# Keys and values in three shared 8 KB buffers, gate tiles in the gate buffer, steps 2 and 3 reordered

## The chip, the cores and the metric

The kernel runs on one core of a Trainium2 chip. The metric is the device time of one execution in microseconds (us), the median of several runs. PE is the matrix engine (PEld its weight loads), DVE the vector engine, ACT the scalar engine, POOL the GpSimd engine, SP the queue that issues nearly all DMAs.

## What is computed

Three layers in a row, all in float32:

```
# 1: gated linear attention (mLSTM): batch 2, 8 heads, 768 tokens, head size 40; per token t
m_new  = max(f[t] + m, i[t])
f_stab = exp(f[t] + m - m_new);  i_stab = exp(i[t] - m_new)
C = f_stab * C + i_stab * v[t] k[t]^T          # 40 x 40 state per head
n = f_stab * n + i_stab * k[t]
y[t] = sigmoid(o[t]) * (C q[t]) / max(|n q[t]|, 1)
# 2: soft mixture of experts: x = y as 1536 x 320, 8 experts of 4 slots, hidden size 1024
logits = x @ phi                                # 1536 x 32
slot_input = softmax(logits over tokens).T @ x  # 32 x 320
slot_out[e] = relu(slot_input[e] @ w1[e]) @ w2[e]
x = softmax(logits over slots) @ slot_out
# 3: four experts weighted by domain_probs
out = sum_e p[:, e] * (relu(x @ u1[e]) @ u2[e])
```

## The kernel before

**Layer 1, the attention.** The 768 tokens of each batch are cut into 6 chunks of 128. A token tile i (0 to 11) is chunk `c = i // 2` of batch `b = i % 2`. The recurrence becomes matmuls inside a tile plus a state that goes from chunk to chunk (`state[b]`, one per batch). The order is written out by hand (`manual_schedule`): each engine does its instructions in the order of the code. Tiles 0 and 1 stand in straight code (lines 700 to 771), tiles 2 to 11 in a loop (lines 774 to 884); pass i of the loop is called step i. The stages of a tile that matter here:

- `stage_S` (L337): scores from transposed queries and keys, `stage_E` (L287, L290): decay weights, `stage_mask` (L296, POOL): the triangle, `stage_W` (L343, DVE): their product.
- `stage_P1` (L361): weights times values. `stage_P2` (L353): queries times state. `stage_T2` (L370), `stage_T1` (L377, L379) add them up on DVE; `stage_G`, `stage_N`, `stage_D` normalise and gate (L424, L384 to L387, L430).
- `stage_Wk` (L323, POOL): weighted keys, `stage_V` (L405): their product with the values into the PSUM bank `kv`, `stage_V1` (DVE): that sum into the state, as a copy (L419) for chunk 0 and as an addition (L417) later. `stage_U` (L393, POOL) decays the state.
- `stage_KT` (L304) transposes the keys of tile i+2 in step i. `stage_X` (L438) and `stage_XC` (L443, ACT) transpose the layer's output of tile i-2 for layer 2.
- The gates of chunks 2 and 3 are worked out in steps 1 and 2 by `gates1a` (two scans L602 and L608 with L605 and L606 between), `gates1b` (L625, L628, L633), `gates2` (L648, L650), those of chunks 4 and 5 in steps 3 to 6. `tokT`, `tokC`, `tokM` (L657 to L681) bring them into columns by token.

**Loads.** In step i SP issues the keys of tile i+3, one or two output gates, values of tile i+2 and some rows of the expert weights w1, in the order of the code. Keys, values, output gates and the first queries are loaded per tile as 128 tokens x 8 heads x 40 floats: 1,024 pieces of 160 bytes, 160 KB. Keys go into `kb[i % 4]` with 64 floats per head (24 of padding), values into `vb[i % 4]` with 41 floats per head (a column of ones for the normaliser), output gates into `x1` without gaps. A DMA waits until the eighth before it has landed (eight landing counters, DMAHW0 to 7), and until its target is free.

**Buffers.** `big` has 11 slots of 10 KB. Seven are first taken by `gin` (raw gates), `gt0`, `gt1`, `gt2` (gate work), `qx` (padded queries) and `x1` of the two batches; the tiles w1_0 to w1_3 take the other four, and w1_4 to w1_7, then w2_1, w2_3, w2_5, w2_7 those that come free, in this order. The tiles w2_0, w2_2, w2_4, w2_6 (`slot3`) lie over the memory of the attention's own pools, `ap` and `attw`.

**Layers 2 and 3.** After step 11 the slots are gathered and `ffn1` (L1139, w1) and `ffn2` (L1179, w2) run; SP meanwhile issues the rest of w1, sixteen loads of w2 (L99, 640 KB each) and the first weights of layer 3, u1a, u1b, u2 (L104, L105, L111). Layer 3 begins with `G_mm` (L1248), which needs u1a and u1b, and is then matmuls on PE until the end (L1292, L1308).

Of the kernel before, what the change touches and what calls it, by code (L numbers as in the profile page):

```python
# [8 lines left out]
F32 = mybir.dt.float32  # L9
# [13 lines left out]
def tile_mlstm_soft_moe_domain_moe(  # L23
# [19 lines left out]
    L = 128  # L43
# [15 lines left out]
    def bc(i):  # L59
        return i % B, i // B  # L60
# [4 lines left out]
    def slot(shape, name, dt=F32):  # L65
        return big.tile(shape, dt, tag="w", name=name)
# [58 lines left out]
    with tc.manual_schedule():  # L125
# [10 lines left out]
        with ExitStack() as actx:  # L136
# [1 line left out]
            wp = actx.enter_context(tc.tile_pool(name="attw", bufs=2, side="right", reuse_waits="tile"))  # L138


            NB = 4
            kb = [ap.tile([128, H, 64], F32, name=f"kb{i}") for i in range(NB)]
            wkb = [ap.tile([128, H, 64], F32, name=f"wkb{i}") for i in range(2)]


            EL = ap.tile([128, S], F32R, name="EL")
            ER = ap.tile([128, 4, HP, L], F32R, name="ER")
            eA = ap.tile([128, NC, 4, HP], F32, name="eA")
            wB = ap.tile([128, NC, 4, HP], F32, name="wB")
            dec = ap.tile([128, NC, B, HP], F32, name="dec")  # L150
            rmask = ap.tile([128, 24], F32, name="rmask")
            vb = [ap.tile([128, H * (D + 1) + 24], F32, name=f"vb{i}") for i in range(NB)]
            state = [ap.tile([128, HP, 2, D + 1], F32, name=f"state{i}") for i in range(2)]

            def vbh(i):
                return vb[i % NB][:, 0:H * (D + 1)].rearrange("p (h d) -> p h d", d=D + 1)


            gin = slot([128, 2, S], "gin")[0:16]
            gt0 = slot([128, 3, S], "gt0")  # L160
            gt1 = slot([128, 3, S], "gt1")
            gt2 = slot([128, 3 * S + 256], "gt2")
# [25 lines left out]
            def load_k(i):  # L188
                b, c = bc(i)
                nc.sync.dma_start(  # L190
                    out=kb[i % NB][:, :, 0:D],
                    in_=k[b, :, c * L:(c + 1) * L, :].rearrange("h p d -> p h d"),
                )

            def load_v(i):
                b, c = bc(i)
                nc.sync.dma_start(
                    out=vbh(i)[:, :, 0:D],
                    in_=v[b, :, c * L:(c + 1) * L, :].rearrange("h p d -> p h d"),
                )  # L200

# [24 lines left out]
            def pairs(t):  # L226
                return t.rearrange("p (g j) d -> p g j d", j=2)
# [73 lines left out]
            def stage_KT(i, pt=None):  # L301
                pK[i] = pt = tr() if pt is None else pt
                for g in range(HP):
                    nc.tensor.transpose(pt[:, g, :], kb[i % NB][:, 2 * g:2 * g + 2, :], ident)  # L304

            def stage_KC(i):
                pt = pK.pop(i)
# [12 lines left out]
            def stage_Wk(i):  # L320
                b, c = bc(i)
                if c < NC - 1:
                    nc.gpsimd.tensor_tensor(  # L323
                        out=pairs(wkb[i % 2])[:, :, :, 0:D], in0=pairs(kb[i % NB])[:, :, :, 0:D],
                        in1=by_head(wB, i, D), op=ALU.mult)

            pS = {}
# [29 lines left out]
            def stage_P1(i):  # L357
                p1 = bank("p1").rearrange("p (h d) -> p h d", d=64)
                for h in range(H):
                    for x in range(2):  # L360
                        nc.tensor.matmul(out=p1[64 * x:64 * x + 64, h, :], lhsT=W[i, h % 2][:, h // 2, 64 * x:64 * x + 64],  # L361
                                         rhs=vb[i % NB][:, h * (D + 1):h * (D + 1) + 64], start=True, stop=True)
                pP[i, 1] = p1

            def stage_T2(i):
# [32 lines left out]
            def stage_V(i):  # L398
                b, c = bc(i)
                if c == NC - 1:  # L400
                    return
                pk = KV[:, 0:HP * (D + 1)].rearrange("p (g d) -> p g d", g=HP)
                for g in range(HP):
                    for j in range(2):
                        nc.tensor.matmul(out=pk[64 * j:64 * j + 64, g], lhsT=wkb[i % 2][:, 2 * g + j, :],  # L405
                                         rhs=vbh(i)[:, 2 * g + j, :], start=True, stop=True)
                pV[i] = pk

            def stage_V1(i):
# [151 lines left out]
            load_q(4)  # L561
            load_v(3)

            nc.gpsimd.memset(kb[0][:, :, D:64], 0.0)
            nc.gpsimd.memset(qb[0][:, :, D:64], 0.0)
            make_identity(nc, ident)
            nc.gpsimd.memset(selR, 1.0)
# [17 lines left out]
            nc.vector.tensor_scalar(mAd, mBd, mA, None, op0=ALU.mult)  # L585
            nc.vector.tensor_scalar(mBd, mBd, mB, None, op0=ALU.mult)

            for t in (kb[1], qb[1], kb[2], qb[2]):
                nc.gpsimd.memset(t[:, :, D:64], 0.0)

            gp = {}
# [74 lines left out]
                nc.scalar.activation(out=wB[:, c0:c1].rearrange("p c q g -> p (c q) g"),  # L666
                                     in_=v[:, :, :, 2, :].rearrange("p c q g -> p (c q) g"), func=AF.Copy)

            def tokM(c0, c1):
                n = c1 - c0  # L670
                pe = KV[:, 3 * L:3 * L + 16 * n]
# [19 lines left out]
            for t in (kb[3], qb[3]):  # L691
                nc.gpsimd.memset(t[:, :, D:64], 0.0)
            nc.gpsimd.memset(sele, 1.0)
            nc.gpsimd.affine_select(out=sele, in_=sele, compare_op=ALU.is_ge, fill=0.0,
                                    base=1 - L, pattern=[[0, 128]], channel_multiplier=1)
            nc.gpsimd.memset(wkb[0][:, :, D:64], 0.0)
            for i, t in enumerate(vb):
                nc.gpsimd.memset(t[:, H * (D + 1):], 0.0)
                nc.gpsimd.memset(vbh(i)[:, :, D:D + 1], 1.0)
            gate_rows(1, 0, 1, KV, 0)  # L700
            gate_rows(0, 0, 1, fgs, 0)
            nc.scalar.activation(out=Ig[:, 0:L], in_=KV[:, 0:L], func=AF.Copy)
# [51 lines left out]
            stage_O(0)  # L754
            stage_P1(0)
            stage_T2(0)
            gates1a(2, 4, Fg[:, 2 * L:4 * L])
            stage_E(2)
            stage_V(0)
            stage_Wk(1)  # L760
            tokM(1, 2)
            stage_T1(0)
            stage_V1(0)
            stage_mask(2)
            stage_O(1)
            load_k(4)
# [7 lines left out]
            for i in range(2, NT):  # L774
# [20 lines left out]
                stage_W(i, 1)  # L795
                if i == 2:
                    gates1b(2, 4, 0, 0)
                    gates1b(2, 4, 0, 1)
                stage_U(i)
                stage_P1(i - 1)  # L800
                stage_T2(i)
                if i + 1 < NT:
                    stage_mask(i + 1)
                if i == 2:
                    stage_V(1)
                    stage_K(3)
                    stage_G(0)
                    stage_N(0)
                    stage_V1(1)
                    nc.gpsimd.memset(x1[0][:, :, DM:384], 0.0)  # L810
                    nc.gpsimd.memset(x1[0][:, :, DM:DM + 1], 1.0)
                    stage_D(0)
                    qT_mm(3, 0)
                    qT_copy(3, 0)
                    gates_hi(2, 4)
                    gates1b(2, 4, 1)
# [19 lines left out]
                for x in qt_work.get(i, []):  # L836
                    qT_mm(*x)
                    qT_copy(*x)
                stage_X(i - 2)
                stage_O(i)  # L840
                stage_V1(i)
                stage_G(i - 1)
# [50 lines left out]
            vfl = vb[iL % NB]  # L893
# [509 lines left out]
```

## Time and profile before

| | us |
|---|---|
| runs before | 326.27, 326.80, 328.74; median 326.8 |
| the profiled execution, its own time | 327.14 |
| its span, first to last instruction | 325.4 |
| PE busy | 312.7 (96%) |
| DVE, ACT, POOL busy | 172.3, 116.9, 91.6 |
| DMA queue of SP | 42.99 MB in 65,392 packets |

One execution was profiled. Of PE, "busy" is the modelled time of pipelined matmuls, so it doesn't say that PE works at its peak. DMA share is the mean busy share of the core's 16 DMA engines; packets can overlap on an engine, so it goes over 1. "Granted clock" is the share of full clock that PE got.

### The profile page before, as it was taken

Reading aid. Unit: us, or ns where it says so; the run is one execution under the profiler, and the core shown is the slowest. Engines: PE = TensorE matmul, PEld = TensorE weight load, DVE = VectorE, ACT = ScalarE, POOL = GpSimd, SP = SyncE. Lnnn points to the kernel's source line nnn. Section 1 sums busy time; section 2 is a strip of 40 time slices with the busy share of each in tenths; the row PEclk is TensorE's granted clock in tenths of the full one; section 3 lists DMA queues with packets and bytes.
Section 4 is the critical chain, followed back from the end, with each engine's and each line's share of the span. In section 5 each row is a group of like instructions: output and inputs, shape, how many; then the busy total and the mean of one; then the engine's idle time right before and its main releaser. Section 6 shows DMA issues by size and latency. Waiting matters only on the chain.

```text
span 325.4 us, 7054 instructions
## 1 busy us (share of the span) xinstructions
PE 312.7 (96%) x2884; PEld 273.4 (84%) x2884; DVE 172.3 (53%) x381; ACT 116.9 (36%) x248; POOL 91.6 (28%) x148
## 2 busy tenths in 40 slices
PE   8988999989999978999999999999999999999995
PEld 7776988768763437899999998999998999999994
DVE  6699899778627124564444444444443444444411
ACT  3676767654311124442223332222223332222200
POOL 6457577555402008750002800002900000000000
PEclk9999999999979999999999999999999999999999
DMA  9999999999999999127200001290000200011111
GB/s 115 154 212 188 222 231 227 218 235 332 305 407 414 412 256 276 45 56 243 84 2 0 2 0 26 52 311 2 0 2 20 47 0 0 22 41 42 40 62 41
DMA packets 65456, 43.49 MB, mean 134 GB/s; under 512 B 49776, under 2 KB 56944, under 8 KB 65424
## 3 DMA queue, kind: packets, MB, share of 16 engines
q1 hardware_dynamic: 65392, 42.99, 50.9%
q8 instruction: 23, 0.38, 0.5%
q14 instruction: 9, 0.07, 0.1%
q10 hardware_dynamic: 32, 0.05, 0.0%
HBM read 39.49 MB, written 1.97 MB: 127 GB/s over the span
## 4 chain that ended last, share of the span: by engine, by line
PE 83%; DMA 6%; DVE 3%; ACT 2%; POOL 2%; issue 1%; SPq 1%; DVEq 0%; POOLq 0%; ACTq 0%
PE po L1308 52%; PE pa L1292 7%; DMA u1b<-in_moe_w_dram 5%; PE pss L337 3%; PE ph L1139 3%; PE p L353 2%; PE p L361 2%; PE pg L1248 2%; DMA kb<-in_k_dram 1%; PE p L537 1%; PE pt L287 1%; PE kvp L949 1%; SPq L91 1%; PE pt L304 1%; PE pt L261 1%
## 5 line engine op out<-in xcount | busy, mean ns | idle before, releaser
L1308 PE MATMUL po<-uh,hh 128*128 128x320 f32 x768 | 170.2, 309 | 0.6 <-ACT hh L1297 0.6
L1308 PEld LDWEIGHTS po<-uh,hh 128*128 128x128 f32 x768 | 131.8, 188 | 5.9 <-POOL ul L1235 1.0
L1308 PE MATMUL po<-ul,hh 128*128 128x320 f32 x384 | 118.3, 309 | 0.0
L1298 DVE SCALAR_TENSOR_TENSOR hh<-pa,hh 128x512 fp32r<-128x512 f32 x96 | 65.8, 691 | 95.4 <-ACT hh L1297 95.4
L1297 ACT ACTIVATE hh<-pa 128x512 fp32r<-128x512 f32 x96 | 56.6, 598 | 121.7 <-PE pa L1292 120.5
L1308 PEld LDWEIGHTS po<-ul,hh 128*128 128x128 f32 x384 | 72.0, 188 | 0.0
L1233 POOL TENSOR_SCALAR uh<-u 128x640 fp32r<-128x640 f32 x16 | 11.6, 726 | 93.4 <-PE po L1308 73.3
L1292 PE MATMUL pa<-cS,gs 128*128 128x512 f32 x96 | 37.0, 398 | 0.3 <-ACT gs L1286 0.3
L1235 POOL TENSOR_TENSOR ul<-u,uh 128x640 fp32r<-128x640 f32 x16 | 25.1, 1569 | 1.3
L1316 DVE SCALAR_TENSOR_TENSOR acc<-po,pr,acc 128x320 f32<-128x320 f32 x36 | 19.6, 543 | 10.6 <-PE po L1308 10.6
L1292 PEld LDWEIGHTS pa<-cS,gs 128*128 128x128 f32 x96 | 17.9, 188 | 1.3 <-ACT gs L1286 0.5
L296 POOL TENSOR_SCALAR_AFFINE_SELECT w<-w 128x512 f32<-128x512 f32 x24 | 15.8, 683 | 6.4 <-ACT w L290 6.2
L343 DVE TENSOR_TENSOR w<-w,pss 128x512 f32<-128x512 f32 x24 | 15.4, 682 | 3.2 <-PE pss L337 3.1
L337 PE MATMUL pss<-qT,kT 64*128 64x128 f32 x192 | 14.9, 297 | 0.0
L290 ACT ACTIVATE w<-pt 128x512 f32<-128x512 f32 x24 | 13.0, 598 | 3.9 <-PE pt L287 3.9
L337 PEld LDWEIGHTS pss<-qT,kT 64*128 64x128 f32 x192 | 12.6, 198 | 2.1 <-issue 0.9
L361 PE MATMUL p<-vb,w 128*64 128x64 f32 x352 | 12.1, 222 | 0.0
L361 PEld LDWEIGHTS p<-vb,w 128*64 128x64 f32 x352 | 11.3, 138 | 0.2 <-issue 0.2
L430 POOL TENSOR_TENSOR x<-x,rd 128x320 f32<-128x320 f32 x11 | 8.4, 764 | 10.7 <-DVE rd L387 9.4
L1179 PE MATMUL po<-w,hT 128*32 128x320 f32 x128 | 10.4, 435 | 1.0 <-DMA w<-in_moe_w_dram 1.0
L1139 PE MATMUL ph<-w,lhs 128*32 128x512 f32 x80 | 10.2, 638 | 0.0
L1179 PEld LDWEIGHTS po<-w,hT 128*32 128x32 f32 x128 | 4.4, 109 | 6.3 <-DMA w<-in_moe_w_dram 2.0
(278 smaller groups left out, 321.0 us busy)
## 6 DMA issues: line engine op xcount, KB each, us to landing
w<-in_moe_w_dram SPq DMA_DIRECT2D x40, 256.0 KB, 5.0
w<-in_moe_w_dram SPq DMA_DIRECT2D x16, 640.0 KB, 10.8
u1a<-in_moe_w_dram SPq DMA_DIRECT2D x4, 1024.0 KB, 11.0
u<-in_moe_w_dram SPq DMA_DIRECT2D x3, 1280.0 KB, 8.9
kb<-in_k_dram SPq DMA_DIRECT2D x12, 160.0 KB, 4.7
vb<-in_v_dram SPq DMA_DIRECT2D x12, 160.0 KB, 5.1
x<-in_o_gate_dram SPq DMA_DIRECT2D x12, 160.0 KB, 4.7
out_dram<-acc SPq DMA_DIRECT2D x12, 160.0 KB, 1.8
```

Source lines behind the costliest of these rows:

```text
L296: nc.gpsimd.affine_select(out=w, in_=w, compare_op=ALU.is_ge, fill=0.0, base=0, pattern=[[0, HP], [1, L]], channel_multiplier=-1)
L337: nc.tensor.matmul(out=pss[j][:, g, :], lhsT=kT[i][64 * j:64 * j + 64, g, :], rhs=q_of(i)[64 * j:64 * j + 64, g, :], start=True, stop=True)
L343: nc.vector.tensor_tensor(out=w, in0=w, in1=pS.pop((i, j)), op=ALU.mult)
L361: nc.tensor.matmul(out=p1[64 * x:64 * x + 64, h, :], lhsT=W[i, h % 2][:, h // 2, 64 * x:64 * x + 64], rhs=vb[i % NB][:, h * (D + 1):h * (D ...
L1139: nc.tensor.matmul(out=ph[32 * j:32 * j + 32, :], lhsT=lhs1[:, r, j, :], rhs=w1s[u, j][:, r, :], start=(r == 0), stop=(r == 4))
L1179: nc.tensor.matmul(out=pos[hf][32 * j:32 * j + 32, 0:DM], lhsT=hT[:, r, 32 * j:32 * j + 32], rhs=w2s[2 * j + hf][:, r // R2, r % R2, :], s ...
L1235: nc.gpsimd.tensor_tensor(out=lo[:, r0:r0 + 2], in0=raw[:, r0:r0 + 2], in1=hi[:, r0:r0 + 2].bitcast(F32), op=ALU.subtract)
L1292: nc.tensor.matmul(out=pa, lhsT=GS[e][0][:, ft * 128:(ft + 1) * 128], rhs=cS[:, tg * 512:(tg + 1) * 512], start=True, stop=True)
L1297: nc.scalar.activation(out=hi, in_=pa, func=AF.Relu)
L1298: nc.vector.scalar_tensor_tensor(out=lo, in0=pa, scalar=0.0, in1=hi.bitcast(F32), op0=ALU.max, op1=ALU.subtract)
L1308: nc.tensor.matmul(out=po[:, 0:DM], lhsT=x[:, sl], rhs=y[e][:, ft, :], start=(ft == 0 and n == 0), stop=(ft == FT - 1 and n == 2))
L1316: nc.vector.scalar_tensor_tensor(out=dst, in0=po[:, 0:DM], scalar=pr[:, i, e:e + 1], in1=dst, op0=ALU.mult, op1=ALU.add)
```

## The change

Four edits:

1. Keys and values. Four key buffers of 2 KB and four value buffers of 1.4 KB per partition become three buffers `kvb` of 8 KB, each with keys and values of both batches for one chunk (`c % 3`). A value row takes 64 floats per head, as a key row does. `stage_P1` reads 64 columns per head from there, as before from 41 + 23 of the next head.
2. Small gate tiles. `state`, `eA`, `wB`, `dec` and `rmask` are cut out of the slot of the raw gates, which becomes `gs0`; that slot is now held until step 11. The slots that w1_4 to w1_7 and w2_1 take move on by one.
3. Fills on POOL. The ones and the padding of the values are filled per buffer, those of the third buffer after the state.
4. Order. Before the loop `tokM(1, 2)` gets a PSUM bank of its own, the state copy of tile 0 goes ahead of `stage_T1(0)`, and the second scan of `gates1a(2, 4)` behind it. In step 2 the state copy of tile 1 goes ahead of half of `gates1b`, `stage_T2(2)`, `stage_G(0)` and `stage_N(0)`; the transposes of tile 0's output go to the end of step 3.

```
-            NB = 4
-            kb = [ap.tile([128, H, 64], F32, name=f"kb{i}") for i in range(NB)]
+            NB = 3
+            kvb = [ap.tile([128, 2, B, H, 64], F32, name=f"kvb{i}") for i in range(NB)]
...
-            eA = ap.tile([128, NC, 4, HP], F32, name="eA")
...
-            vb = [ap.tile([128, H * (D + 1) + 24], F32, name=f"vb{i}") for i in range(NB)]
-            state = [ap.tile([128, HP, 2, D + 1], F32, name=f"state{i}") for i in range(2)]
...
-            gin = slot([128, 2, S], "gin")[0:16]
+            def kb(i):
+                b, c = bc(i)
+                return kvb[c % NB][:, 0, b]
+
+            def vb(i):
+                b, c = bc(i)
+                return kvb[c % NB][:, 1, b]
...
+            gs0 = slot([128, 2560], "gs0")
+            gin = gs0[0:16, 0:2 * S].rearrange("p (y s) -> p y s", y=2)
+            used = [2 * S]
+
+            def part(n):
+                used[0] += n
+                return gs0[:, used[0] - n:used[0]]
+
+            state = [part(2 * HP * (D + 1)).rearrange("p (g j d) -> p g j d", g=HP, j=2) for _ in range(2)]
+            eA = part(NC * 16).rearrange("p (c q g) -> p c q g", c=NC, q=4)
...
-                    out=vbh(i)[:, :, 0:D],
+                    out=vb(i)[:, :, 0:D],
...
-                                         rhs=vb[i % NB][:, h * (D + 1):h * (D + 1) + 64], start=True, stop=True)
+                                         rhs=vb(i)[:, h, :], start=True, stop=True)
...
-            for i, t in enumerate(vb):
-                nc.gpsimd.memset(t[:, H * (D + 1):], 0.0)
-                nc.gpsimd.memset(vbh(i)[:, :, D:D + 1], 1.0)
+            for t in kvb[0:2]:
+                nc.gpsimd.memset(t[:, 1, :, :, D + 1:64], 0.0)
+                nc.gpsimd.memset(t[:, 1, :, :, D:D + 1], 1.0)
...
+            nc.gpsimd.memset(kvb[2][:, 0, :, :, D:64], 0.0)
+            nc.gpsimd.memset(kvb[2][:, 1, :, :, D + 1:64], 0.0)
+            nc.gpsimd.memset(kvb[2][:, 1, :, :, D:D + 1], 1.0)
...
-            gates1a(2, 4, Fg[:, 2 * L:4 * L])
+            gates1a(2, 4, Fg[:, 2 * L:4 * L], (0, 1))
             stage_E(2)
             stage_V(0)
             stage_Wk(1)
-            tokM(1, 2)
+            tokM(1, 2, bank("p2"))
+            stage_V1(0)
             stage_T1(0)
-            stage_V1(0)
+            gates1a(2, 4, Fg[:, 2 * L:4 * L], (2,))
...
                 if i == 2:
                     gates1b(2, 4, 0, 0)
-                    gates1b(2, 4, 0, 1)
                 stage_U(i)
                 stage_P1(i - 1)
-                stage_T2(i)
+                if i > 2:
+                    stage_T2(i)
...
                 if i == 2:
                     stage_V(1)
                     stage_K(3)
+                    stage_V1(1)
+                    gates1b(2, 4, 0, 1)
+                    stage_T2(i)
                     stage_G(0)
                     stage_N(0)
-                    stage_V1(1)
...
-                stage_X(i - 2)
+                if i > 2:
+                    stage_X(i - 2)
...
-                stage_XC(i - 2)
+                if i > 2:
+                    stage_XC(i - 2)
+                if i == 3:
+                    stage_X(0)
+                    stage_XC(0)
```

On SP's queue, in steps 8 and 9 (the waits are the counters of the eight landings, and engines named for a buffer that must come free; w1 are the expert weights, vb and kvb the values), before:

```order
L197 DMA vb2_102<-in_v_dram 128x8x40 [waits DMAHW6_49,PE_49]
L91 DMA w1_4_1005<-in_moe_w1_dram 128x512 [waits DMAHW7_49]
L91 DMA w1_5_1118<-in_moe_w1_dram 128x512 [waits DMAHW0_49,DVE_49]
L91 DMA w1_5_1118<-in_moe_w1_dram 128x512 [waits DMAHW1_49]
L91 DMA w1_5_1118<-in_moe_w1_dram 128x512 [waits DMAHW2_49]
L197 DMA vb3_103<-in_v_dram 128x8x40 [waits DMAHW3_49,PE_49]
L91 DMA w1_5_1118<-in_moe_w1_dram 128x512 [waits DMAHW4_49]
L91 DMA w1_5_1118<-in_moe_w1_dram 128x512 [waits DMAHW5_49]
L91 DMA w1_6_1232<-in_moe_w1_dram 128x512 [waits DMAHW6_49,DVE_49]
```

The same place in the changed kernel:

```order
L208 DMA kvb2_90<-in_v_dram 128x8x40 [waits DMAHW6_49,PE_49]
L91 DMA w1_4_994<-in_moe_w1_dram 128x512 [waits DMAHW7_49]
L91 DMA w1_5_1107<-in_moe_w1_dram 128x512 [waits DMAHW0_49,DVE_49]
L91 DMA w1_5_1107<-in_moe_w1_dram 128x512 [waits DMAHW1_49]
L91 DMA w1_5_1107<-in_moe_w1_dram 128x512 [waits DMAHW2_49]
L208 DMA kvb2_90<-in_v_dram 128x8x40 [waits DMAHW3_49,PE_49]
L91 DMA w1_5_1107<-in_moe_w1_dram 128x512 [waits DMAHW4_49]
L91 DMA w1_5_1107<-in_moe_w1_dram 128x512 [waits DMAHW5_49]
L91 DMA w1_6_1221<-in_moe_w1_dram 128x512 [waits PE_49,DMAHW6_49,Activation_49,Pool_49]
```

No load has moved; w1_6 now waits for the last readers of another slot (`gt2`).

On DVE, at the end of the straight code ahead of step 2 (gt_108 is `gt1`, L379 the copy of tile 0's P1, L419 the copies of state 0), before:

```order
L606 TENSOR_TENSOR gt_108<-gt_108,gt_107 128x256
L608 SCALAR_TENSOR_TENSOR gt_108<-gt_108 128x256
L674 TENSOR_TENSOR wB<-kv,wB 128x16
L379 COPY t_352<-p_335 128x328
L419 COPY state_104<-kv 64x4x41 x2
L343 TENSOR_TENSOR w<-w,pss 128x512 x2
```

Now, with line numbers of the changed kernel (L617 is L606, L619 is L608, L685 is L674, L430 is L419, L390 is L379, L354 is L343):

```order
L617 TENSOR_TENSOR gt_97<-gt_97,gt_96 128x256
L685 TENSOR_TENSOR gs_95<-p_362,gs_95 128x16
L430 COPY gs_95<-kv 64x4x41 x2
L390 COPY t_340<-p_323 128x328
L619 SCALAR_TENSOR_TENSOR gt_97<-gt_97 128x256
L354 TENSOR_TENSOR w<-w,pss 128x512 x2
```

The second scan has gone from ahead of the token sum and the state copies to behind them.

On DVE in step 2 (L625, L628 and L633 are `gates1b`, L370 is T2 of tile 2, L424 to L387 are G and N of tile 0, L419 the copies of state 1), before:

```order
L625 SCALAR_TENSOR_TENSOR gt_109<-gt_107,rmask,gt_109 128x256
L628 SCALAR_TENSOR_TENSOR gt_109<-gt_108,rmask,gt_109 128x256
L370 TENSOR_TENSOR t_452<-p_422,eA 128x328
L424 SCALAR_TENSOR_TENSOR x_0_111<-x_0_111,t_352 128x320
L384 SCALAR_TENSOR_TENSOR dn<-t_352 128x8
L386 TENSOR_SCALAR dn<-dn 128x8
L387 RECIPROCAL rd<-dn 128x8
L419 COPY state_105<-kv 64x4x41 x2
L633 SCALAR_TENSOR_TENSOR gt_109<-gt_109,rmask 128x256
```

Now:

```order
L636 SCALAR_TENSOR_TENSOR gt_98<-gt_96,gs_95,gt_98 128x256
L430 COPY gs_95<-kv 64x4x41 x2
L639 SCALAR_TENSOR_TENSOR gt_98<-gt_97,gs_95,gt_98 128x256
L381 TENSOR_TENSOR t_460<-p_411,gs_95 128x328
L435 SCALAR_TENSOR_TENSOR x_0_100<-x_0_100,t_340 128x320
L395 SCALAR_TENSOR_TENSOR dn<-t_340 128x8
L397 TENSOR_SCALAR dn<-dn 128x8
L398 RECIPROCAL rd<-dn 128x8
L644 SCALAR_TENSOR_TENSOR gt_98<-gt_98,gs_95 128x256
```

The copies of state 1 have gone ahead of six instructions.

## Rows read from the trace of the kernel before

**Rows 1.** The page, slices: DMA busy tenths in 40 equal slices.

```profile
DMA  9999999999999999127200001290000200011111
```

**Rows 2.** Stretches: length, busy PE PEld DVE ACT POOL (instructions), granted clock, DMA share, GB/s.

```profile
4.60:10.50 5.90, 5.90 (x26) 5.12 (x26) 4.55 (x14) 2.85 (x9) 2.60 (x11) 1.00 1.54 136
10.50:13.40 2.90, 2.90 (x20) 2.24 (x20) 0.70 (x3) 1.44 (x3) 0.77 (x2) 1.00 1.43 174
...
15.70:17.60 1.90, 1.90 (x23) 1.66 (x23) 1.86 (x4) 1.90 (x6) 1.84 (x3) 1.00 1.40 192
...
35.00:72.00 37.00, 35.28 (x618) 29.79 (x618) 31.69 (x82) 25.07 (x61) 23.23 (x35) 1.00 1.00 225
...
91.00:114.00 23.00, 23.00 (x236) 10.82 (x235) 8.36 (x29) 2.81 (x6) 2.08 (x2) 0.93 1.02 415
...
121.20:325.40 204.20, 198.90 (x1336) 189.32 (x1336) 91.06 (x151) 58.84 (x102) 36.36 (x32) 1.00 0.20 58
```

**Rows 3.** The chain that ended last, in order of time: start, us, what.

```profile
60.62 0.75 PE p L353 x16
61.37 0.74 SPq L197
...
65.90 4.68 DMA kb<-in_k_dram
...
105.47 15.76 DMA u1b<-in_moe_w_dram
```

**Rows 4.** Waits of PE, 10 to 125 us: us in total, times, longest.

```profile
PE kv L405 <- POOL x L811: 1.5, 1, 1.5
PE pt L304 <- DMA kb<-in_k_dram: 1.1, 1, 1.1
...
PE p L353 <- DVE state L419: 0.9, 1, 0.9
PE pg L1248 <- DMA u1b<-in_moe_w_dram: 0.6, 1, 0.6
```

**Rows 5.** Waits of SP's queue, 16 to 76 us.

```profile
SPq L197 <- PE p L361: 4.0, 3, 1.8
...
SPq L190 <- POOL w L296: 1.2, 2, 0.9
```

**Rows 6.** Timeline of SP's queue: start, us, engine, line, DMA, count.

```profile
47.40 1.61 SPq L197 DMA_DIRECT2D vb<-in_v_dram  x1
...
73.44 7.89 SPq L91 DMA_DIRECT2D w<-in_moe_w_dram  x11
...
83.95 20.17 SPq L99 DMA_DIRECT2D w<-in_moe_w_dram  x16
...
105.47 0.48 SPq L105 DMA_DIRECT2D u1b<-in_moe_w_dram  x1
```

**Rows 7.** Timeline of PE in steps 4 and 8.

```profile
38.84 1.10 PE L361 MATMUL p<-vb,w 128*64 128x64 f32 x32
...
63.92 1.04 PE L261 MATMUL pt<-ident,qx 128*128 128x128 f32 x8
```

**Rows 8.** POOL's fills of keys and values: ns min/median/max, first and last start, form.

```profile
L589 POOL MEMSET kb<- x2: 247/248/248, 2.5 to 2.9; 128x192 f32 x2
...
L698 POOL MEMSET vb<- x4: 117/118/118, 4.4 to 4.7; 128x24 f32 x4
L699 POOL MEMSET vb<- x4: 112/112/113, 4.4 to 4.7; 128x8 f32 x4
```

**Rows 9.** Timeline around step 2; in brackets idle time before, and releaser.

```profile
20.58 1.00 DVE L608 TENSOR_TENSOR_SCAN gt<-gt 128x256 f32<-128x256 f32 x1
...
22.89 0.79 PE L353 MATMUL p<-state,qT 128*64 128x82 f32 x16 [0.93 <-DVE state L419]
...
26.89 0.61 DVE L419 COPY state<-kv 64x164 f32<-64x164 f32 x2
...
27.61 0.67 PE L405 MATMUL kv<-vb,wkb 128*64 128x41 f32 x16 [1.52 <-POOL x L811]
```

More of the change, by code (lines that the diff above doesn't have):

```diff
@@ L147, in tile_mlstm_soft_moe_domain_moe @@
             ER = ap.tile([128, 4, HP, L], F32R, name="ER")
-            eA = ap.tile([128, NC, 4, HP], F32, name="eA")
-            wB = ap.tile([128, NC, 4, HP], F32, name="wB")
-            dec = ap.tile([128, NC, B, HP], F32, name="dec")
-            rmask = ap.tile([128, 24], F32, name="rmask")
-            vb = [ap.tile([128, H * (D + 1) + 24], F32, name=f"vb{i}") for i in range(NB)]
-            state = [ap.tile([128, HP, 2, D + 1], F32, name=f"state{i}") for i in range(2)]
-            def vbh(i):
-                return vb[i % NB][:, 0:H * (D + 1)].rearrange("p (h d) -> p h d", d=D + 1)
-            gin = slot([128, 2, S], "gin")[0:16]
+            def kb(i):
[12 more added lines that the diff above has]
+            eA = part(NC * 16).rearrange("p (c q g) -> p c q g", c=NC, q=4)
+            wB = part(NC * 16).rearrange("p (c q g) -> p c q g", c=NC, q=4)
+            dec = part(NC * B * HP).rearrange("p (c b g) -> p c b g", c=NC, b=B)
+            rmask = part(24)
             gt0 = slot([128, 3, S], "gt0")
@@ L190, in load_k @@
                 nc.sync.dma_start(
-                    out=kb[i % NB][:, :, 0:D],
+                    out=kb(i)[:, :, 0:D],
                     in_=k[b, :, c * L:(c + 1) * L, :].rearrange("h p d -> p h d"),
@@ L303, in stage_KT @@
                 for g in range(HP):
-                    nc.tensor.transpose(pt[:, g, :], kb[i % NB][:, 2 * g:2 * g + 2, :], ident)
+                    nc.tensor.transpose(pt[:, g, :], kb(i)[:, 2 * g:2 * g + 2, :], ident)
             def stage_KC(i):
@@ L323, in stage_Wk @@
                     nc.gpsimd.tensor_tensor(
-                        out=pairs(wkb[i % 2])[:, :, :, 0:D], in0=pairs(kb[i % NB])[:, :, :, 0:D],
+                        out=pairs(wkb[i % 2])[:, :, :, 0:D], in0=pairs(kb(i))[:, :, :, 0:D],
                         in1=by_head(wB, i, D), op=ALU.mult)
@@ L405, in stage_V @@
                         nc.tensor.matmul(out=pk[64 * j:64 * j + 64, g], lhsT=wkb[i % 2][:, 2 * g + j, :],
-                                         rhs=vbh(i)[:, 2 * g + j, :], start=True, stop=True)
+                                         rhs=vb(i)[:, 2 * g + j, 0:D + 1], start=True, stop=True)
                 pV[i] = pk
@@ L562, in tile_mlstm_soft_moe_domain_moe @@
             load_v(3)
-            nc.gpsimd.memset(kb[0][:, :, D:64], 0.0)
+            nc.gpsimd.memset(kb(0)[:, :, D:64], 0.0)
             nc.gpsimd.memset(qb[0][:, :, D:64], 0.0)
@@ L586, in tile_mlstm_soft_moe_domain_moe @@
             nc.vector.tensor_scalar(mBd, mBd, mB, None, op0=ALU.mult)
-            for t in (kb[1], qb[1], kb[2], qb[2]):
+            for t in (kb(1), qb[1], kb(2), qb[2]):
                 nc.gpsimd.memset(t[:, :, D:64], 0.0)
@@ L667, in tokC, with tokM @@
                                      in_=v[:, :, :, 2, :].rearrange("p c q g -> p (c q) g"), func=AF.Copy)
-            def tokM(c0, c1):
+            def tokM(c0, c1, t=None):
                 n = c1 - c0
-                pe = KV[:, 3 * L:3 * L + 16 * n]
+                pe = KV[:, 3 * L:3 * L + 16 * n] if t is None else t[:, 0:16 * n]
                 nc.tensor.matmul(out=pe, lhsT=sele, rhs=eA[:, c0:c1].rearrange("p c q g -> p (c q g)"), start=True, stop=True)
@@ L690, in tile_mlstm_soft_moe_domain_moe @@
             fill(6, wz)
-            for t in (kb[3], qb[3]):
+            for t in (kb(3), qb[3]):
                 nc.gpsimd.memset(t[:, :, D:64], 0.0)
@@ L892, in tile_mlstm_soft_moe_domain_moe @@
             x1L = x1_of(iL)[:, 0:DM].rearrange("p (h d) -> p h d", d=D)
-            vfl = vb[iL % NB]
+            vfl = vb(iL)
             pa_ = bank("p1").rearrange("p (h d) -> p h d", d=64)
@@ L905, in last_p @@
                                          lhsT=W[iL, h % 2][:, h // 2, 64 * x:64 * x + 64],
-                                         rhs=vfl[:, h * (D + 1):h * (D + 1) + 64], start=True, stop=True)
+                                         rhs=vfl[:, h, :], start=True, stop=True)
             def last_d(h0, h1, p1, step, eng):
```

## Prediction

> **What bounds the kernel now.** I read the slices of the whole span first. The DMA engines are at 9 tenths in the first sixteen slices, to about 130 us, and almost idle afterwards [rows 1]. So there are two regimes, and the table of stretches gives each its limit [rows 2]. From 121.2 us to the end PE is busy 198.90 of 204.20 us at full clock with DMA at 0.20: a PE stage of about 204 us that starts when its operands are there. From 91 to 114 us the DMA engines move 415 GB/s at a share of 1.02: weights at the transfer limit. From 35 to 72 us they are at 1.00 again, but move 225 GB/s, since keys, values and output gates come in pieces of 160 bytes.
>
> The chain of waits names what starts the last stage: the load u1b, issued at 105.47 and waited for 15.76 us [rows 3]; PE idles 0.6 us for it [rows 4]. A 256 KB load takes that long only behind others. SP issues the sixteen w2 loads over 20.17 us, and u1b directly after them [rows 6]. Above u1b the chain shows PE, then the load of the last keys (k(11), 65.90 to 70.58), then SP and the matmuls P2 [rows 3]. I don't follow it there yet, because a wait for several semaphores is put down to the one that came last.
>
> The question is whether the stream of loads ever waits for compute. The list of SP's waits says so: value loads waited 4.0 us for L361 and key loads 1.2 us for a mask [rows 5]. Take the value load issued at 47.40 for 1.61 us [rows 6]. It is v(7), issued in step 5, and it reuses the buffer of v(3), whose last reader is P1(3). That is the L361 burst at 38.84, over at 39.94 [rows 7], 7.5 us before. The semaphore had long been reached, and the 1.61 us were back-pressure of the transfers. The other loads are alike: with four buffers, k(i+3) and v(i+2) reuse what a step before i has read. So up to 94 us the stream runs at its own pace and compute follows. PE idles 1.08 us for k(11) [rows 4], and the page's "PE first, then u1b" is two engines that both trail one stream.
>
> So I make the sum for the stream: whatever is added to or taken from the transfers before u1b lands moves the 204 us behind it one for one. What only PE, DVE or POOL gain before that ends in a longer wait for k(10), k(11) or u1b.
>
> **The change part by part.**
>
> *Values at 64 floats per head.* The number of pieces is unchanged: twelve value loads of 1,024 pieces of 160 bytes. Only the distance of the rows in SBUF goes from 164 to 256 bytes, that of keys and early queries. The start of the trace has stretches in which one kind lands almost alone [rows 2]. From 4.60 to 10.50 it is keys and queries: 136 GB/s, so 163,840 bytes take 1.205 us. From 10.50 to 13.40 it is v(0), o(0), v(1): 174 GB/s, 0.94 us each. From 15.70 to 17.60 o(1) and v(2): 192 GB/s, 0.85 us. Output gates lie without gaps. By these rows a load costs the more the further its rows stand apart, and a value load at 256 bytes becomes a key load. I take 1.2 against 1.0 us (1.0 because in the 174 GB/s stretch the two value loads share the mean with a gapless one): 0.2 us for each of twelve, 2.4 us. Upper end: values cost the 0.85 us of the fastest stretch now and all of 1.205 later, 12 x 0.355 = 4.3 us. Lower end: between weight loads the distance doesn't matter, 0. Below nothing: aligned rows are better and values reach the 0.85 us, 12 x (0.94 - 0.85) = 1.1 us gained.
>
> On this the Trainium skill has a rule, in "DMA: Bandwidth & Descriptors", section "How a descriptor splits into AXI transactions": a piece that doesn't start on a 256-byte boundary is cut at one and costs extra beats. By it rows at 256 bytes are the best case, and the change saves time; the rows above say the contrary, since keys, already at 256 bytes, are the slowest (136 GB/s).
>
> *Three shared buffers for four and four.* The reuse of a key or value slot goes from four loads back to six. The order of SP's queue doesn't change (first pair of order rows), so no load is asked for earlier; only waits go that had already been met. Worth 0. If they were real, it would be the 4.0 + 1.2 us of [rows 5]: a rival.
>
> *Gate tiles in the gate buffer.* One weight slot that used to come free in step 2 is held until step 11, so w1_4 to w1_7 take gt0, gt1, gt2 and qx. SP issues eleven of the loads of w1_5 to w1_7 from 73.44 to 81.33 [rows 6]. The last reader of qx is the transpose at 63.92 [rows 7], those of gt2 are in step 6, earlier still. Cover of 9 us or more, cost 0. If it went, every microsecond of SP's wait would count once the eight outstanding loads had drained.
>
> *More filling on POOL.* Eight fills of 117 and 112 ns go, 0.92 us [rows 8]. In come two of 128x368 before the first mask, two of 128x16, and three for the last buffer; from 248 ns for 128x192 [rows 8] I estimate 0.45 us per large one, some 2.1 us together, 1.2 us net. POOL is busy 2.60 of 5.90 us there [rows 2], and nothing on it is due before the first mask. Cost 0.
>
> *Reorder in steps 2 and 3.* Before, the copies of state 0 stand behind the scan L608 (1.00 us) and the copy L379, and P2(2) on PE waits 0.93 us for them; V(2) waits 1.52 us for bank kv, which the copies L419 of state 1 free at 27.50, not the POOL fill that the view names [rows 4, 9]. The second and third order rows put both copies forward. PE can gain up to 0.93 + 1.52 = 2.45 us around 22 to 28 us; against that, the gate work for step 4 moves back behind the copies, about 0.6 us. I expect some 1 to 2 us on PE by 30 us, and 0 at the end: late in the loop PE meets the key loads. Transposing x of token tile 0 one step later needs it only in step 6: 0.
>
> Sum: 327.14 us of the profiled execution + 2.4 = 329.5. The median of the runs is 0.34 us lower, so **329.2 us**. About 1% of 326.8, or 3.3 us, is what a measurement of this kernel can tell from no change; the forecast lies inside.
>
> **Rivals.**
> - *The distance costs nothing* in the mixed stretch (35 to 72 us, weights between the small loads): 326.8 us. For: there the share is 1.00, not 1.54, so the limit may be another. Against: four of the twelve loads lie in the pure stretch at the start.
> - *The front gain reaches the end.* If the chain is right that P2 in step 8 released a load, the 1 to 2 us of the reorder go through SP to k(11) and on: about 325.3 us. Against: the met semaphores above, and DMA at 1.00.
> - *Aligned rows land faster*: value loads reach the 0.85 us of the fastest stretch, 326.8 - 1.1 = 325.7 us. Against: keys at 136 GB/s. This is the mechanism of the Trainium skill's rule in "DMA: Bandwidth & Descriptors", section "How a descriptor splits into AXI transactions".
> - *Buffer waits were real*: the list's 5.2 us leave the stream, 321.6 us. Decides only if a load's semaphore is reached after SP comes to it.
> - *Slower by over 1%*: the whole gap between fastest and key-like loads is paid on each value load, 326.8 + 4.3 = 331.1 us. It decides if the slowest of the 16 engines, which a load must await, feels the distance as the start of the trace does; from 0.28 us a load on, twelve loads pass 3.3 us. For: the steady 136 GB/s. Against: with weights between, engines have other work to overlap.
>
> **How the numbers follow.** Forecast (+2.4, own range 328.2 to 330.0) 0.42; distance free 0.22; front gain 0.12; aligned faster 0.07; real buffer waits 0.05; slower by over 1% 0.12. Faster by over 1% is the buffer rival and a little of what combines two gains: 0.06. Slower takes its own rival and the upper edge of the forecast, 0.12 + 0.05 = 0.17. Within 1%: 0.77. The range goes from 325.2 (front gain and alignment) to 331.1 (the upper bound).
>
> **What would show it.** In the changed kernel the stretch in which v(0), o(0) and v(1) land should fall from 174 towards 145 GB/s; u1b should land at 122.5 to 124 us for 121.2; PE should wait 3 us or more for key loads where it waits 1.08; the last stage should stay at 204 us. The waits of P2(2) and V(2) for state copies should shrink. The forecast is wrong in its cause if value loads move at 170 GB/s or more, and wrong in its structure if u1b lands earlier than 121 us while the small loads are no faster: then the stream did wait for compute.

## The result, and the profile after

The changed kernel takes 323.1 us against 326.7 (medians of 14 runs each): a ratio of 0.9891, 95% interval 0.9856 to 0.9925, some 3.6 us faster. I had forecast 329.2 us and a range from 325.2. The time lies below the range, and the sign is wrong.

The execution that was profiled first took 327.89 us, the longest of the 14, so I read a second one, of 322.71 us (span 320.8 us), the run called e2 below. Against it stands a second execution of the kernel before, 325.85 us (span 324.1 us), called e1.

The stretches, with the columns of [rows 2]. The kernel before, again (e1):

```profile
4.60:10.50 5.90, 5.18 (x44) 4.14 (x45) 4.69 (x15) 3.58 (x11) 2.81 (x12) 1.00 1.55 136
10.50:13.40 2.90, 2.90 (x29) 2.10 (x27) 2.83 (x7) 2.88 (x8) 2.60 (x4) 1.00 1.42 174
...
35.00:72.00 37.00, 31.85 (x579) 26.80 (x580) 28.71 (x73) 22.44 (x54) 23.11 (x34) 1.00 0.98 221
91.00:114.00 23.00, 23.00 (x243) 10.95 (x246) 8.07 (x28) 2.48 (x5) 2.08 (x2) 0.93 1.02 413
119.00:324.10 205.10, 199.87 (x1353) 189.72 (x1352) 91.75 (x152) 59.98 (x105) 36.33 (x32) 1.00 0.20 60
```

The changed kernel (e2):

```profile
4.60:10.50 5.90, 5.90 (x26) 5.12 (x26) 4.54 (x14) 2.85 (x9) 3.77 (x13) 1.00 1.08 188
10.50:13.40 2.90, 2.90 (x24) 2.12 (x23) 0.70 (x3) 1.44 (x3) 0.77 (x2) 1.00 1.06 184
...
35.00:72.00 37.00, 35.58 (x621) 29.93 (x621) 30.25 (x80) 25.23 (x61) 22.48 (x34) 1.00 0.91 223
91.00:114.00 23.00, 23.00 (x259) 10.54 (x257) 8.55 (x30) 2.98 (x7) 2.08 (x2) 1.00 1.01 379
115.80:320.80 205.00, 199.92 (x1353) 189.73 (x1352) 91.78 (x152) 60.02 (x105) 36.29 (x32) 1.00 0.19 58
```

Three things are to be seen. The last stage is 205.1 and 205.0 us long: nothing was gained there, it only starts 3.2 us earlier (`G_mm` at 118.99 and 115.82). The first stretch, where before almost only keys and queries land, went from 136 to 188 GB/s, though no one touched their layout, and its DMA share fell from 1.55 to 1.08: less engine time for more bytes. And from 35 to 72 us PE is busy 35.58 us; in e1 it was 31.85, with long waits for keys. That difference is mostly e1's own: in the execution of [rows 2] PE was busy 35.28 us there and waited 1.1 us for keys [rows 4]. The waits of PE before (e1), from 2 to 125 us:

```profile
PE pt L304 <- DMA kb<-in_k_dram: 4.9, 3, 1.8
PE kv L405 <- POOL x L811: 1.5, 1, 1.5
PE p L353 <- DVE state L419: 0.9, 1, 0.9
```

In the changed kernel the three are gone, and no load is among the longest; in place of them stand (10 to 125 us):

```profile
PE pt L298 <- DVE ER L661: 1.7, 1, 1.7
PE pt L298 <- ACT xT L454: 0.8, 1, 0.8
```

Landings, from the trace's landing events (the last of a load's 16), in us: the fourth value load 20.8 before (e1) and 16.6 after (e2), the last keys 71.2 and 65.5, the last w2 114.4 and 110.0, u1b 119.6 and 115.0. So the loads of e2 gain some 4 us in the first 17 us, keep it, and 3.2 us of it reach the last stage.

### The profile page after: what moved, and what is told of

The parts are those of the page before. It is cut to its first block, busy times and chain, and to the rows that moved or that the text cites. A ratio compares the mean times of both kernels' runs of the same rounds, so it can differ in the third digit from the quotient of the medians.

```text
span 326.1 us, 7041 instructions
## 1 busy us (share of the span) xinstructions
PE 316.3 (97%) x2884; PEld 276.8 (85%) x2884; DVE 170.4 (52%) x381; ACT 117.2 (36%) x248; POOL 91.8 (28%) x147
## 4 chain that ended last, share of the span: by engine, by line
PE 89%; DVE 4%; DMA 2%; ACT 1%; issue 1%; POOL 1%; SPq 1%; DVEq 0%; ACTq 0%; POOLq 0%
PE po L1330 52%; PE pa L1314 7%; PE pss L348 4%; PE ph L1161 3%; PE po L1201 3%; PE p L372 2%; PE pg L1270 2%; PE p L364 2%; PE pt L298 2%; DMA w<-in_moe_w_dram 1%; PE p L548 1%; PE kvp L971 1%; DMA x<-in_o_gate_dram 1%; PE pt L272 1%; PE kv L416 1%
## 5 line engine op out<-in xcount | busy, mean ns | idle before, releaser
L354 DVE TENSOR_TENSOR w<-w,pss 128x512 f32<-128x512 f32 x24 | 15.4, 682 | 5.8 <-PE pss L348 5.7
L348 PE MATMUL pss<-qT,kT 64*128 64x128 f32 x192 | 16.0, 312 | 0.0
L348 PEld LDWEIGHTS pss<-qT,kT 64*128 64x128 f32 x192 | 13.5, 210 | 2.3 <-issue 0.8
L372 PE MATMUL p<-kvb,w 128*64 128x64 f32 x352 | 13.0, 230 | 0.0
L372 PEld LDWEIGHTS p<-kvb,w 128*64 128x64 f32 x352 | 12.1, 146 | 0.2 <-issue 0.2
L298 PE MATMUL pt<-ER,EL 32*128 32x512 f32 x24 | 7.1, 542 | 2.3 <-DVE ER L661 1.7
L1201 PE MATMUL po<-w,hT 128*32 128x320 f32 x128 | 9.2, 434 | 0.0
```

The lines of the kernel that those rows point to most:

```text
L348: nc.tensor.matmul(out=pss[j][:, g, :], lhsT=kT[i][64 * j:64 * j + 64, g, :], rhs=q_of(i)[64 * j:64 * j + 64, g, :], start=True, stop=True)
L354: nc.vector.tensor_tensor(out=w, in0=w, in1=pS.pop((i, j)), op=ALU.mult)
L1201: nc.tensor.matmul(out=pos[hf][32 * j:32 * j + 32, 0:DM], lhsT=hT[:, r, 32 * j:32 * j + 32], rhs=w2s[2 * j + hf][:, r // R2, r % R2, :], s ...
```

## The experiments

Theory C: compute of the attention reaches the end, so the reorder pays. Theory L: the loads are faster by the layout. A third, theory R, was that the early stretch differs from execution to execution. Each ratio below is against executions of the kernel before that were taken together with the run, and has a 95% interval.

**e1 and e2: both kernels once more, unchanged.**

> The kernel before, unchanged, for a second profiled execution. Theory L (the early loads are faster because of the layout): the stretch from 4.60 to 10.50 us moves 136 GB/s again, within 8. Theory R (that stretch differs from execution to execution): it can be anything from 130 to 185 GB/s, and u1b lands anywhere within 2 us of 121.2.

> The changed kernel, unchanged, for a profiled execution near its median of 323.1 us. Theory C (the compute of the attention reaches the end): the end of the last attention tile and the landing of u1b both come 2 to 4 us earlier than before, the last stage stays at 204 us. Theory L (faster loads alone): small loads at over 240 GB/s from 35 to 72 us where before had 225, and PE waits less for keys. Rival: the gain lies in the last stage, which would fall to about 200 us with the start unchanged.

e1 moved 136 GB/s again: it is no accident of one execution. e2, 322.9 us, ratio 0.9915 (0.988 to 0.995), gave the rows above. The last stage did not shrink, and the attention's last product (L904, L926) ends 1.0 us earlier only (81.24 and 80.28), while u1b lands 4.6 us earlier. Theory C wanted both 2 to 4 us earlier, so it does not hold as stated. Of Theory L, PE's shorter wait for keys came, but the 240 GB/s did not: 35 to 72 us stayed at 223.

**e3 and e4: the two halves of the change.** e3 is the kernel before with edit 4 alone, e4 the changed kernel without it. The edit of e3, shortened:

```
-            gates1a(2, 4, Fg[:, 2 * L:4 * L])
+            gates1a(2, 4, Fg[:, 2 * L:4 * L], (0, 1))
...
-            tokM(1, 2)
+            tokM(1, 2, bank("p2"))
+            stage_V1(0)
             stage_T1(0)
-            stage_V1(0)
+            gates1a(2, 4, Fg[:, 2 * L:4 * L], (2,))
```

> The kernel before with the reorder of steps 2 and 3 alone; buffers, layout and gate tiles as before. Theory C: most of the 3.6 us is here, 323.0 to 324.5 us. Theory L: 326 to 327.5 us, within 1 us of before, and PE meets the same waits for key loads.

> The changed kernel with the old order of steps 2 and 3: three shared buffers, values at 64 floats per head, gate tiles in the gate buffer. Theory C: 326 to 327.5 us. Theory L: 323 to 324.5 us, and the first 10 us of loads at about 180 GB/s. My prediction's term (values cost 0.2 us more each): 328 to 330 us.

Measured: e3 326.1 us, ratio 0.9993 (0.9963 to 1.0023); e4 323.2 us, 0.9916 (0.9882 to 0.9949). The layout is the whole gain, the order none of it. The first stretch of e3 and of e4 (whose profiled execution, 325.3 us, is the longest of its eight):

```profile
4.60:10.50 5.90, 5.90 (x26) 5.12 (x26) 4.54 (x14) 2.85 (x9) 2.60 (x11) 1.00 1.55 137
```

```profile
4.60:10.50 5.90, 5.90 (x26) 5.12 (x26) 4.54 (x14) 2.85 (x9) 3.77 (x13) 1.00 1.10 190
```

**e5 to e8: what in the layout.** Keys kept their 64 floats per head and became faster. What changed for them is where their buffers begin in SBUF, the on-chip memory that the loads fill (addresses within a partition, from the built programs). In the kernel before, key buffers start 192 bytes and the early query buffers 224 bytes past a multiple of 256 bytes. With rows 256 bytes apart, each piece of 160 bytes then crosses such a line (192 + 160 = 352). Values at 164 bytes cross with 5 or 4 of 8 pieces, output gates with 4 of 8. In the changed kernel the pools have other sizes, and the shared buffers start 32, the early queries 64 bytes past a line: of keys, queries and values no piece crosses. Theory B is that the crossing costs. e5 adds one unused tile to the kernel before, which moves its keys, early queries and values by 128 bytes (of the values 4 or 5 of 8 pieces still cross):

```
             state = [ap.tile([128, HP, 2, D + 1], F32, name=f"state{i}") for i in range(2)]
+            pad = ap.tile([128, 32], F32, name="pad")
```

e6 adds one of 96 bytes to the changed kernel, which puts keys, values and queries where keys and queries lay before; e7 one of 32 bytes (8 in place of 24), which starts keys and values on the lines:

```
             ER = ap.tile([128, 4, HP, L], F32R, name="ER")
+            pad = ap.tile([128, 24], F32, name="pad")
```

e8 is e6 with each key load cut in two, even heads and odd heads:

```
+                for x in range(2):
+                    nc.sync.dma_start(
+                        out=kb(i)[:, x::2, 0:D],
+                        in_=k[b, x::2, c * L:(c + 1) * L, :].rearrange("h p d -> p h d"),
+                    )
```

> The kernel before with one unused tile of 128 bytes per partition at the end of the attention's pool, which moves the start of the key and early query buffers from 192 and 224 to 64 and 96 bytes past a 256-byte line, so that no piece of 160 bytes crosses one; the value rows stay at 164 bytes, with half of their pieces across. Theory B (a piece that crosses a 256-byte line of SBUF costs double): keys and queries land every 0.75 to 0.9 us instead of 1.2, packets of 14 ns instead of 29 in the first 10 us, u1b 2 to 4 us earlier, 322.5 to 324.5 us. Rival S (the sharing of keys and values in one buffer, or fewer buffers, speeds the loads): 325.5 to 327 us, keys at 1.2 us.

> The changed kernel with one unused tile of 96 bytes per partition, which puts the shared buffers and the early queries at 192 and 224 bytes past a 256-byte line, where keys and queries lay before; every piece of keys and values crosses a line. Theory B: 327 to 330 us, keys and values both at 1.2 us a load in the first 14 us (this would be my forecast's sum, with the line and not the distance as its cause). Rival S: as the changed kernel, 322.5 to 323.5 us.

> The changed kernel with one unused tile of 32 bytes per partition: keys and values start on 256-byte lines, the early queries 32 bytes past one; no piece crosses. Theory B (only crossing counts): as the changed kernel, 322.5 to 323.5 us and 180 to 190 GB/s in the first 10 us. Rival A (the start must lie on a line to be cheapest): 1 us or more faster, packets under 14 ns.

> The same buffers as with the 96-byte shift, and each key load cut in two DMAs, even heads and odd heads. Pieces of even heads cross a 256-byte line that is no 512-byte line, those of odd heads cross a 512-byte line. If every 256-byte line costs, both halves take about 0.6 us; if only 512-byte lines do, the even half takes 0.4 and the odd half 0.8 us. Its time is not of interest.

e5: 323.3 us, ratio 0.9897 (0.9855 to 0.9938). One unused tile gives the kernel before the whole gain. e6: 327.6 us, 1.0034 (1.0007 to 1.0061). All four edits of the change together, with the buffers across the lines, are slightly slower than before. Both lie in theory B's ranges and outside rival S's. The first two stretches of e5 and of e6:

```profile
4.60:10.50 5.90, 5.90 (x26) 5.12 (x26) 4.54 (x14) 2.85 (x9) 2.60 (x11) 1.00 1.04 177
10.50:13.40 2.90, 2.90 (x23) 2.12 (x21) 0.70 (x3) 1.43 (x3) 0.76 (x2) 1.00 1.14 198
```

```profile
4.60:10.50 5.90, 5.90 (x26) 5.12 (x26) 4.54 (x14) 2.85 (x9) 3.77 (x13) 1.00 1.55 136
10.50:13.40 2.90, 2.90 (x26) 2.13 (x25) 0.71 (x3) 1.45 (x4) 0.78 (x2) 1.00 1.51 151
```

The same two layouts, each at either speed: 136 GB/s belongs to the position, not to the kernel. The list of DMA issues from 1 to 13 us (kind, count, size, median us from issue to landing) says it per load; e5, then e6:

```profile
kb<-in_k_dram SPq DMA_DIRECT2D x4, 160.0 KB, 3.4
vb<-in_v_dram SPq DMA_DIRECT2D x4, 160.0 KB, 3.7
```

```profile
kvb<-in_k_dram SPq DMA_DIRECT2D x4, 160.0 KB, 5.0
kvb<-in_v_dram SPq DMA_DIRECT2D x2, 160.0 KB, 5.3
```

By the medians of their 16 landings, the first two value loads of e6 land 1.13 and 1.24 us after the load ahead of them, in e1 0.99 and 1.05, in e2 0.77 and 0.85: with all pieces, half and none of them across. In e5, with half across as in e1, the two are 0.82 and 0.99 us: between half and none these gaps alone do not decide.

e7 moved the same bytes in the first stretches as e2:

```profile
4.60:10.50 5.90, 5.90 (x26) 5.12 (x26) 4.54 (x14) 2.85 (x9) 3.77 (x13) 1.00 1.04 179
10.50:13.40 2.90, 2.90 (x23) 2.12 (x21) 0.71 (x3) 1.44 (x3) 0.77 (x2) 1.00 1.04 182
```

Starting on the line is no better than starting 32 bytes behind it. Its median was 325.4 us, ratio 0.9946 (0.991 to 0.998), a miss, above what I expected: four executions took 322.6 to 322.9 us, one 324.9, and five about 326.1 with a mean granted clock of 0.984 where the profiled one has 0.993. The changed kernel has such executions too, 4 of its 24 (326.05 to 326.11 us, 0.984). Why e7 has more of them is open.

e8: the even and odd halves of the second, third and fourth key load land 0.60 and 0.60, 0.61 and 0.60, 0.59 and 0.60 us after the load ahead. Every 256-byte line costs, not only each second one. (By the addresses it is the even heads that cross the 512-byte lines, the other way round than I had expected; both are alike.) Lines of 128 bytes cannot be the cause: each piece crosses exactly one multiple of 128 in every layout here. Its time, 326.8 us, is that of a single execution.

**e9 to e11: does compute set the end now?** PE's longest wait in e2 is for ER, the gate work of chunks 2 and 3 (L661). e9 puts it ahead of tile 1's sums in step 2, e10 does the same to e3, so with loads across the lines; e11 is e9 with the transposes of tile 0's output back in step 2.

```
                     gates_hi(2, 4)
                     gates1b(2, 4, 1)
+                    gates2(2, 4, (A_, V_, V_, G_, A_))
...
-                    gates2(2, 4, (A_, V_, G_, G_, A_))
```

> The changed kernel, and in step 2 the last gate work for chunks 2 and 3 (the decay rows ER and EL that the scores of tile 4 need) goes ahead of the sums, state and normaliser of tile 1, two of its four parts on DVE and one on POOL. That takes away PE's longest wait of the attention, 1.7 us for ER. Theory C (in the changed kernel the loads are early enough, and PE's own chain through the attention sets the end): 320 to 322 us, tile 5's scores start 1.5 to 3 us earlier than 43.2 us. Rival (the loads still set the end): 322.5 to 323.5 us with the same landing of u1b.

> The same edit on the kernel before with the reorder alone, so with keys and queries across 256-byte lines. Theory (there the stream of loads sets the end): as before within 0.3 per cent, 325 to 326.5 us; what PE gains at 30 us ends in a longer wait for keys or for u1b. Rival (PE sets the end there too): 323 to 324.5 us.

> As the kernel before this one (changed kernel with the gate work for chunks 2 and 3 earlier), and the transposes of tile 0's output back in step 2, which takes one of the two copies xT out of ACT's queue where PE waited 1.8 us for it. Theory C (compute sets the end of the changed kernel): scores of tile 5 start before 42 us, no fall of the clock between 34 and 44 us, 320 to 322 us. Rival (the loads, or a new wait in the same place, take the gain back): 322.5 to 324.5 us.

e10: 326.0 us, 1.0005 (0.9975 to 1.0036), as expected. Its profiled execution is the clearest case: PE has full clock from 13 to 323 us, tile 5's scores start at 41.73 us for 43.85 in e3, and the execution still takes 326.7 us. What PE won ends in longer waits for loads:

```profile
PE po L1187 <- DMA w<-in_moe_w_dram: 2.1, 3, 1.2
PE pt L304 <- DMA kb<-in_k_dram: 2.0, 3, 1.0
PE pt L287 <- ACT xT L443: 1.8, 1, 1.8
```

e9: 324.3 us, 0.9922 (0.9894 to 0.9951), a miss. In its profiled execution, 324.75 us and the longest of seven (three took 322.8 to 322.9 us), tile 4's scores start 2.25 us earlier (34.16 for 36.41), and tile 5's 1.65 us later than in e2 (44.81). A new wait takes the place of the old, and the clock falls after it:

```profile
PE pt L298 <- ACT xT L454: 1.8, 1, 1.8
```

```profile
35.00:37.00 2.00, 0.75 (x7) 0.31 (x5) 1.90 (x6) 0.70 (x4) 0.43 (x1) 1.00 1.01 236
37.00:39.00 2.00, 1.43 (x11) 1.00 (x13) 0.42 (x1) 1.97 (x6) 0.99 (x2) 0.55 1.00 277
39.00:44.00 5.00, 5.00 (x67) 4.92 (x64) 2.60 (x9) 1.21 (x2) 2.62 (x4) 0.50 0.94 216
```

The wait alone does not explain the loss: e10 has the same one (last line of its list) and keeps full clock.

e11: 323.3 us, 0.9897 (0.9857 to 0.9937), above the 320 to 322 us that I expected. In its profiled execution, 324.4 us and the longest of six, PE waits 1.6 us for POOL in the same place, tile 5's scores start at 42.70, and the clock falls in two other places (30.5 and 92 us). No version here beats the changed kernel.

## Why the prediction was wrong

**What bounds the kernel: right for the kernel before, not for the changed one.** Before, the stream of loads set the start of the last stage, and the last stage kept its length. e10 shows it from the side of PE, e5 from the side of the loads: 128 bytes nobody reads, no instruction moved, 1.0% faster. "One for one" was too much: u1b came 4.6 us earlier and the last stage 3.2, since PE becomes the limit on the way (below).

**Values at 64 floats per head: the step that failed.** I read 136, 174 and 192 GB/s [rows 2] as a price of the distance between rows, and the three cases fitted. They fit as well with the share of pieces that cross a 256-byte line: all of them in the first stretch, about half in the other two. Distance and position were mixed up in the rows, and I had not worked out where the buffers begin. So the term had the wrong sign for values (1.0 us before, about 0.8 now, for 1.2 forecast), and keys and early queries, which I left out because their layout does not change, gained more: 163,840 bytes at 136 GB/s take 1.20 us, at 188 GB/s 0.87. Moving the pools had moved them. Where the forecast's case holds, its sign is right and its size about double: in e6 the values cost about what keys cost (1.13 and 1.24 us), and that kernel, with all the edits, is 0.34% (about 1.1 us) slower, for 2.4 us forecast.

The rival of aligned rows named the right kind of mechanism and gave it too little, 1.1 us, for values alone. I put it aside because keys lie 256 bytes apart already; but 256 bytes apart and 192 bytes off, every one of them crosses. The Trainium skill's page "DMA: Bandwidth & Descriptors", section "How a descriptor splits into AXI transactions", cuts a piece at 256-byte boundaries and charges one that does not start on a boundary. It speaks of reads; for these writes to SBUF e8 agrees on the 256 bytes. e7 shows no price of the start by itself: 179 GB/s on the line, 188 and 190 at 32 bytes behind it (e2, e4). That rule of the Trainium skill goes by where a piece starts; the prediction made of it that rows 256 bytes apart are the best case, and left out where the buffer starts.

**What would show it.** I had named 170 GB/s in the stretch of values as the number at which my cause falls; it came to 184. That u1b would land at 122.5 to 124 us and PE wait 3 us or more for keys was wrong with it: 115.0 us and none. The last stage kept its length and the waits of P2(2) and V(2) went, as forecast.

**Three shared buffers, gate tiles, fills: 0, and no run speaks against it.** e4 (323.2 us, ratio 0.9916) and e5 (323.3, 0.9897) differ by all three and by the values' rows, and their intervals overlap. Each by itself they were not tried. That e4 is no faster than e5, though values cross no lines there, fits with compute as the next limit.

**Reorder: 0 at the end, right; on PE, more was won than I thought and all given back.** The scores (L337) of tiles 2, 3 and 4 before, then in e3, with the next wait of PE between (start, us, what):

```profile
20.37 1.16 PE L337 MATMUL pss<-qT,kT 64*128 64x128 f32 x16
...
30.18 1.16 PE L337 MATMUL pss<-qT,kT 64*128 64x128 f32 x16
...
36.69 1.16 PE L337 MATMUL pss<-qT,kT 64*128 64x128 f32 x16
```

```profile
20.46 1.16 PE L337 MATMUL pss<-qT,kT 64*128 64x128 f32 x16
...
27.46 1.16 PE L337 MATMUL pss<-qT,kT 64*128 64x128 f32 x16
30.37 0.53 PE L287 MATMUL pt<-ER,EL 32*128 32x512 f32 x2 [1.74 <-DVE ER L650]
...
37.10 1.16 PE L337 MATMUL pss<-qT,kT 64*128 64x128 f32 x16
```

Tile 3 starts 2.8 us sooner after tile 2 (7.00 for 9.81). Then PE waits 1.74 us for the gate rows that moved back on DVE, the clock falls to half, and tile 4 is as late as before. I had priced that gate work at 0.6 us and stopped at 30 us; the wait sits behind it. So in e3 the zero was luck in its reason: this wait took the gain, not the key loads that I had named. With the wait gone, in e10, the loads take it.

**Where the rest of the loads' lead went.** u1b is 4.6 us earlier and the end 3.2. The stream now does wait for compute. SP's longest waits in the changed kernel (e2, 20 to 110 us):

```profile
SPq L99 <- PE po L1135: 6.6, 1, 6.6
SPq L99 <- PE ph L1161: 3.8, 1, 3.8
SPq L196 <- ACT qx L252: 3.5, 2, 2.2
```

In e1 the wait for `po` was 3.6 us (L1113) and the queries' (L196 here) is not among its longest seven. The weights then move at 379 GB/s from 91 to 114 us, in e1 at 413. And `ffn2` ends 4.2 us after the last w2 has landed, 3.0 before: PE is late there too. `ffn2` takes PE 10.2 us in e2, e5 and e7 alike, 10.8 in e1 and 12.5 in the execution of [rows 2]. PE's first products with u1b come 0.4 us after its landing in e1 and 1.9 us after it in e2; in e1, then in e2:

```profile
119.99 0.64 PE L1248 MATMUL pg<-u1b,lhsG 64*32 64x256 f32 x8
```

```profile
116.83 0.64 PE L1270 MATMUL pg<-u1b,lhsG 64*32 64x256 f32 x8
```

So in e2 PE sets the start of the last stage, no longer a load. Two more executions with the changed layout fit that, the one of 327.89 us and e4's: their fourth value loads land at 17.2 and 16.8 us, near e2's 16.6, but PE did tile 1's scores in 2.08 us for 1.16, and u1b landed at 119.8 and 119.4 us. That an edit which speeds up compute would now reach the end is not shown: e9 and e11 were to show it, and their gains were lost on the way.

## What to carry to other kernels

Work out where a DMA's pieces lie in SBUF, not only how far apart: start plus row distance times index, modulo 256, for every buffer, and count those that cross a line. A change of one pool's size moves the buffers of others, so loads that the diff does not touch belong in the sum; a tile of a few bytes is a cheap test. And a rule fitted to three rows should be asked what else differs between them before it carries a sign.

## What the runs showed of the hardware

- A load of 1,024 pieces of 160 bytes lands every 1.18 to 1.20 us when all its pieces cross a 256-byte line of SBUF, every 0.85 to 0.89 us when none does (medians of the landings from the first keys to the third queries: the execution of [rows 2], e1, e3 and e6 against e2, e4, e5 and e7). The whole first stretch moves 136 or 137 GB/s against 177 to 190, and its DMA share per GB/s is halved: 1.55 for 136 in e1, 1.08 for 188 in e2. All pieces here have 160 bytes, so no run separates crossing a line from starting more than 96 bytes behind one.
- In some executions the clock fell after PE had been short of work. In e2 (26 to 34 us, columns as above) PE is busy 0.26 of 2 us, then has half clock, 1.2 of 2.4 GHz, and DVE's gate work is the cause of the gap:

```profile
26.00:28.00 2.00, 2.00 (x20) 1.49 (x20) 1.90 (x9) 1.97 (x5) 1.37 (x2) 1.00 1.11 271
28.00:30.00 2.00, 0.26 (x4) 0.21 (x2) 1.90 (x6) 0.92 (x4) 2.00 (x4) 0.89 1.01 178
30.00:32.00 2.00, 2.00 (x24) 1.56 (x26) 1.03 (x3) 1.38 (x3) 0.72 (x4) 0.50 0.84 259
```

- It does not always fall. In e10, around its wait of 1.8 us for ACT, PE is busy 0.51 of 2 us and keeps full clock, where e9 fell to half:

```profile
35.00:37.00 2.00, 0.51 (x3) 0.18 (x1) 1.94 (x5) 0.93 (x5) 0.68 (x1) 1.00 0.49 146
37.00:39.00 2.00, 1.68 (x39) 1.44 (x41) 0.51 (x2) 2.00 (x5) 1.04 (x3) 1.00 0.86 210
```

- Where it falls, a wait can cost more than itself: from tile 3's scores to tile 4's it is 9.64 us in e3, with the wait of 1.74 us and the half clock behind it, and 6.84 us in e10 (27.08 to 33.92), with 0.2 us of that wait and full clock.
- In e4's profiled execution the sixteen score matmuls at 11.86 us took 2.08 us, in e2 1.44, and those at 17.75 us still 2.08 (e2: 1.16 at 15.36): PE can start slow and stay so to about 21 us. That execution took 325.3 us for a median of 323.2; that the slow start is the whole reason is not shown.
